# One score product per block and head in the mixed part, and a rewritten set-up of block-sparse attention with a mixture of experts

## The chip, the cores and the metric

The kernel runs on one core of one Trainium2 chip. The metric is the time of one execution on the device in microseconds (us), as the median of several runs. Profiles come from one further execution, whose times are given in us from the start of its span. Engine names are those of the profile: PE is TensorE (PEld its weight loads), DVE VectorE, ACT ScalarE, POOL GpSimd and SP the engine that issues most DMAs.

## The reference

Attention over 4 batches, 8 heads, 768 positions of 64 features, in 24 blocks of 32 positions. A query block sees its own block and both neighbours, the first and the last block, and three sampled blocks; the first and last query block see everything. The result goes, token by token, through four experts with two layers each.

```python
mask = np.abs(blk_i - blk_j) <= window
mask = mask | (blk_i == 0) | (blk_j == 0) | (blk_i == n_blocks - 1) | (blk_j == n_blocks - 1)
for qb in range(n_blocks):
    for kb in sampled_blocks[qb]:
        mask[qb*block:(qb+1)*block, kb*block:(kb+1)*block] = True
attn = softmax(np.where(mask, scale * q @ k.T, -1e9));  x = attn @ v
for e in range(E):
    h = np.maximum(x @ w1[e], 0.0)
    out += p[:, e:e+1] * (h @ w2[e])
```

## The kernel before, in words

**Tiling of the attention.** The 22 inner query blocks of a batch are gathered in groups t of four (the last has two). A group is worked on as two units u of four heads each (class `Group`), so a batch has 12 group units; the first and last query block make four `Edge` units. A query block has eight key slots of 32 positions: three neighbours (its own block and both sides), the first block, three sampled blocks, the last block. `S` (lines 292 to 323) makes the scores. For each head pair `i` and block `c` it multiplies q with the three neighbour slots, read from the batch's key tile `k` (line 304, 96 columns), and then with the other five slots, read from a buffer `kr` (line 309, 160 columns). The two heads of a pair lie in the two halves of the partitions, and the blocks' results in four groups of 32 output partitions, so eight products run side by side. Each float32 product shows as two instructions in the trace. Then DVE reduces scores and mask to a row bound (line 319) and ACT takes the exponential (322). `T` transposes the weights on TensorE (331) and copies them out (333: half on ACT, half on DVE in the set-up). `A` multiplies them with the value rows (359). In the set-up, `A` also divides by the sums (348, 349, 377), and `X` transposes a finished group into tokens (403), which `tokens` splits into high and low parts (281 on ACT, 282 on DVE) as operands of the experts.

**Buffers and loads.** `copy_k` fills the five-slot buffers `kr`: the end blocks by one copy (149), the sampled ones by one copy each (156) on POOL, ACT and DVE in turn (`copier`). Their block numbers are loaded into an engine's register on first use (141). `load_v` fetches value rows: one DMA on SP's queue for the neighbours (175) and an indirect one on POOL's queue per block for the sampled rows (179). `put_ends` copies the end rows into each value tile (852). Expert weights come by SP (580, 585) and are split into high and low parts by ACT and POOL (597 and 598, 611 and 612, 635 and 636).

**Order of the work.** All engines run in the order in which the code issues instructions. The kernel has two parts. The set-up and the first six units of batch 0 (lines 833 to 898) run alone, since the experts need tokens. The mixed part begins with the first expert product (662) and interleaves expert products (662, 683, 732) with the other attention units by planned times (`drive`, `attend`). The planned times depend on constants of the code. In `attend`, unit n's scores are issued in iteration n, its transposes and values in iteration n + 1. The slots of the next group are copied in two portions: one block's in the iteration of the first unit of a group, the other three blocks' in that of the second; there are five `kr` buffers in this part and eight in the set-up.

The mask is made from `bad` (which slots to drop) by one small product with a pattern of 24 x 768 elements, `ind` (239 to 258).

## Time and profile before

| what | value |
|---|---|
| median of 3 runs | 1254.86 us (1254.47 to 1259.41) |
| profiled execution | 1257.47 us, its span 1255.6 us |
| mean granted TensorE clock | 0.995 |
| keys of batch 0: first copies that read them start at | 8.94 us |
| mean of one exponential on ACT (L322, 128x256) | 499 ns |
| starts of score units around a refill of keys, batches 0 and 1 | 115.39 and 127.00; 136.87 and 148.77; 240.51 and 252.57; 264.18 and 274.05; 285.69 and 297.32; 309.67 and 321.30; 332.91 and 342.81 us |
| the closest such pair in batches 2 and 3 | 480.81 and 495.60 us |

How to read it: the span goes from the first to the last instruction; the time of the execution has some 2 us more. A stage in which an engine is busy all the time is bound by that engine. The TensorE clock has two levels here, 1.0 (2.4 GHz) and 0.5 (1.2 GHz). In a row of the timeline, the first number is the start, the second how long the instructions in the row were busy; the time from one row's start to the next is what the work costs when rows follow without idle time.

### The profile page before, as it was taken

To read this page: it belongs to the slowest core of one execution; us is meant where nothing else is said; L and a number is where in the kernel's file an instruction comes from. 1 tells how busy PE (TensorE), PEld (TensorE's weight loads), DVE (VectorE), ACT (ScalarE), POOL (GpSimd) and SP (SyncE) were. 2 spreads that over 40 slices of the span, in tenths; PEclk is the share of its full clock that TensorE was granted. 3 is DMA by queue.
4 is the path that set the end of the run, shared out by engine and by line. 5 is a ranking of instruction groups with operands and counts; after the bars stand their busy time and mean duration, and the time that the engine had idled before them with its cause. 6 is when DMAs were issued, how large, how long until landed. Compare 5 with 4: busy or idle time off the path is not lost.

```text
span 1255.6 us, 31597 instructions
## 1 busy us (share of the span) xinstructions
PE 1231.8 (98%) x12242; PEld 1072.5 (85%) x12242; DVE 753.9 (60%) x1735; ACT 679.5 (54%) x1826; POOL 719.0 (57%) x848
## 2 busy tenths in 40 slices
PE   6899999999999999999999999999999999999998
PEld 4788888888888888888888888888888899999997
DVE  6455535555458675666658676665756855555553
ACT  5556645666655546666555455666664544444441
POOL 6566556666659545555547655556544855555550
PEclk9899999999999999999999999999999999999999
DMA  9546555655535325332323433333321222222211
GB/s 258 181 128 170 153 183 170 192 174 173 159 111 188 110 68 156 98 118 90 111 86 120 145 102 100 103 119 114 118 77 43 93 93 67 68 68 68 67 51 51
DMA packets 64113, 149.02 MB, mean 119 GB/s; under 512 B 7707, under 2 KB 9244, under 8 KB 63964
## 3 DMA queue, kind: packets, MB, share of 16 engines
q1 hardware_dynamic: 58294, 129.70, 32.9%
q0 software_dynamic: 5632, 17.31, 5.1%
q8 instruction: 96, 1.57, 0.5%
q14 instruction: 53, 0.43, 0.1%
q10 hardware_dynamic: 38, 0.00, 0.0%
HBM read 140.69 MB, written 6.29 MB: 117 GB/s over the span
## 4 chain that ended last, share of the span: by engine, by line
PE 67%; DVE 1%; issue 1%; POOL 0%; POOLq 0%; DVEq 0%
PE po L732 33%; PE w L683 16%; PE v L683 12%; PE o L359 2%; PE tp L331 1%; PE s L309 1%; PE s L304 1%; DVE oacc L747 1%; PE ow L469 1%; PE sw L418 1%; PE tw L440 0%; DVE r L619 0%; POOL wo L612 0%; DVE r L617 0%; PE v L662 0%
## 5 line engine op out<-in xcount | busy, mean ns | idle before, releaser
L612 POOL TENSOR_TENSOR wo<-r,wo 128x256 fp32r<-128x256 f32 x288 | 241.1, 840 | 279.7 <-ACT wo L611 278.1
L732 PE MATMUL po<-h,hh 128*128 128x512 f32 x768 | 310.2, 404 | 1.3 <-DVE oacc L747 1.1
L732 PE MATMUL po<-h,hl 128*128 128x512 f32 x768 | 302.6, 394 | 0.0
L732 PE MATMUL po<-l,hh 128*128 128x512 f32 x768 | 301.7, 393 | 0.0
L683 PE MATMUL w<-xo,wo 128*128 128x384 f32 x1152 | 236.1, 340 | 0.0
L636 POOL TENSOR_TENSOR l<-r,h 128x512 fp32r<-128x512 f32 x160 | 211.4, 1321 | 37.5 <-ACT h L635 37.0
L683 PEld LDWEIGHTS w<-xo,wo 128*128 128x128 f32 x1152 | 207.5, 188 | 18.0 <-DVE z L718 0.7
L683 PE MATMUL v<-xo,wo 128*128 128x384 f32 x864 | 175.9, 338 | 0.0
L732 PEld LDWEIGHTS po<-h,hl 128*128 128x128 f32 x768 | 144.2, 188 | 33.0
L683 PEld LDWEIGHTS v<-xo,wo 128*128 128x128 f32 x864 | 154.4, 188 | 12.3 <-ACT z L710 0.2
L732 PEld LDWEIGHTS po<-h,hh 128*128 128x128 f32 x768 | 144.2, 188 | 19.6 <-DVE oacc L747 2.9
L598 POOL TENSOR_TENSOR wo<-r,wo 128x256 fp32r<-128x256 f32 x128 | 95.3, 747 | 114.7 <-ACT wo L597 109.3
L732 PEld LDWEIGHTS po<-l,hh 128*128 128x128 f32 x768 | 145.2, 189 | 11.4
L611 ACT CAST wo<-r 128x256 fp32r<-128x256 f32 x288 | 114.5, 398 | 49.7 <-PE w L683 32.2
L747 DVE SCALAR_TENSOR_TENSOR oacc<-po,pr,oacc 128x512 f32<-128x512 f32 x168 | 124.3, 742 | 24.6 <-PE po L732 24.4
L322 ACT ACTIVATE p<-p,mx 128x256 f32<-128x256 f32 (+1 forms) x192 | 95.5, 499 | 69.4 <-DVE mx L319 67.5
L635 ACT CAST h<-r 128x512 fp32r<-128x512 f32 x160 | 99.3, 620 | 11.8 <-PE po L732 11.8
L179 POOL DMA_INDIRECT v<-in_vr_dram,vidx x88 | 85.7, 974 | 26.3 <-issue 16.6
L319 DVE CUSTOM_DVE_ANT_1 p<-s,mask 128x256 f32<-128x256 f32 (+1 forms) x192 | 69.9, 418 | 46.3 <-PE s L309 45.9
L662 PE MATMUL v<-xo,wo 128*128 128x384 f32 x384 | 79.9, 345 | 0.5 <-ACT xo L281 0.5
L706 DVE TENSOR_TENSOR p<-w,p 128x384 f32<-128x384 f32 x48 | 26.7, 556 | 89.4 <-PE w L683 82.3
L662 PE MATMUL w<-xo,wo 128*128 128x384 f32 x384 | 79.1, 341 | 0.0
(139 smaller groups left out, 1723.4 us busy)
## 6 DMA issues: line engine op xcount, KB each, us to landing
r<-in_w_dram SPq DMA_DIRECT2D x80, 512.0 KB, 4.0
r<-in_w_dram SPq DMA_DIRECT2D x160, 256.0 KB, 2.7
v<-in_vr_dram SPq DMA_DIRECT2D x44, 384.0 KB, 4.8
k<-in_kb_dram SPq DMA_DIRECT2D x8, 768.0 KB, 5.7
v<-in_vr_dram SPq DMA_DIRECT2D x12, 512.0 KB, 5.1
out_dram<-oacc SPq DMA_DIRECT2D x23, 256.0 KB, 2.5
q<-in_qb_dram SPq DMA_DIRECT2D x20, 256.0 KB, 5.2
v<-in_vr_dram SPq DMA_DIRECT2D x24, 128.0 KB, 3.4
```

What stands on the lines that cost most here:

```text
L179: nc.gpsimd.indirect_dma_start(out=v[:G, i, 1], out_offset=None, in_=vr, element_offset=b * S * DM, in_offset=bass.IndirectOffsetOnAxis(ap ...
L319: nc.vector.tensor_tensor_reduce(p.rearrange("p (a b) -> p a b", b=BLOCK), s[h][:n, i], mk, -SCALE, 3.0e38, ALU.add, ALU.min, mx[:n])
L322: nc.scalar.activation(p, p, AF.Exp, bias=mx[:n], scale=-1.0, accum_out=self.sums[:n, m:m + 1])
L598: nc.gpsimd.tensor_sub(o[:, 1], r[s][:, i, k], f32(o[:, 0]))
L611: nc.scalar.copy(o[:, 0], src)
L612: nc.gpsimd.tensor_sub(o[:, 1], src, f32(o[:, 0]))
L635: nc.scalar.copy(h, r)
L636: nc.gpsimd.tensor_sub(l, r, f32(h))
L662: nc.tensor.matmul(W[s], w[:, wi, t], x[xi][:, k * KH + t], start=k == 0 and m == 0, stop=k == 1 and m == 3 * KH - 1)
L683: nc.tensor.matmul(ps, w[:, wi, t], x[:, xi, t], start=fresh and m == 0, stop=m == 3 * KH - 1, skip_group_check=not fresh)
L732: nc.tensor.matmul(p, a[:, js], w, start=f == 0 and n == 0, stop=f == FT - 1 and n == 2)
L747: nc.vector.scalar_tensor_tensor(accs[tok], p, pe, accs[tok], op0=ALU.mult, op1=ALU.add)
```

## The change

In the mixed part a `kr` buffer has all eight slots: the three neighbours come by a DMA of their own on SP's queue, and `S` makes one product of 256 columns for a block and head. There are four such buffers instead of five, and the slots of all four blocks of the next group are filled in the iteration of the group's second unit. The five-slot form and two products stay in the first six units. There, keys of four blocks lie in one buffer (two of them), with one copy for all end blocks; block numbers are loaded early; ACT and POOL do most sampled copies; the end rows are copied by halves of the heads. `S` and `soft` are split, so that TensorE's instructions of an iteration come before the softmax of the same unit, and the half copy of the unit before lies between the exponentials. Division (`G`) and token split (`C`) are issued after the softmax. The third group's value loads come ahead of the second w1 load and the w2 loads. The mask is made by two smaller products. Some small tiles have fewer buffers, and the edge queries share the ring of the q tiles and are loaded in the mixed part.

```diff
-        return nc.scalar if j <= QG and r == 2 else COPIERS[r % len(COPIERS)]
+        if first_units[0]:
+            if j <= QG:
+                return (nc.gpsimd, nc.scalar, nc.vector if j % 2 else nc.scalar)[r]
+            return nc.gpsimd if (j + r) % 2 else nc.scalar
+        return COPIERS[r % len(COPIERS)]
...
+    def read_blocks(t, eng):
+        for j in blocks(t):
+            for r in range(NR):
+                if copier(j, r) is eng:
+                    sampled_block(j, r)
...
     def copy_k(b, t, cs=range(QG)):
         for c, j in enumerate(blocks(t)):
             if c in cs:
+                w = pool["slots"] - NR - 2
...
                 k = keep("k", make)
+                if w:
+                    nc.sync.dma_start(k[:, :w], kb[b, :, j - 1:j + 2])
...
-                    copy(k[:, 1 + r:2 + r], keys[b][0][:, bass.ds(sampled_block(j, r), 1)])
+                    copy(k[:, w + 1 + r:w + 2 + r], keys[b][0][:, bass.ds(sampled_block(j, r), 1)])
...
+    def group_keys(t):
+        ks = kept.get(t % 2) or pool["k"].tile([P, QG, NR + 2, P], F32, name="kr")
+        if t < 2:
+            kept[t] = ks
+            nc.vector.tensor_copy(ks[:, :, 0:NR + 2:NR + 1],
+                                  keys[0][0][:, 0:NB:NB - 1].unsqueeze(1).broadcast_to([P, QG, 2, P]))
+        gathered[0, t][1].update((c, ks[:, c]) for c in range(QG))
...
-    for c in range(QG):
-        for r in (1, 2):
-            sampled_block(1 + c, r)
+    for t in range(2):
+        read_blocks(t, nc.scalar)
...
                     for h, half in enumerate(halves):
-                        nc.tensor.matmul(s[h][cs, i, :3], q[half, c, e], k[half, j - 1:j + 2, e],
-                                         start=True, stop=True)
-                for c, j in enumerate(blocks(t)):
+                        if whole:
+                            nc.tensor.matmul(s[h][cs, i], q[half, c, e], ks[c][half, :, e],
+                                             start=True, stop=True)
+                        else:
+                            nc.tensor.matmul(s[h][cs, i, :3], q[half, c, e], k[half, j - 1:j + 2, e],
+                                             start=True, stop=True)
+                for c, j in enumerate(() if whole else blocks(t)):
...
+                if i == 0 and between:
+                    between()
...
-        renew(2 * QG, 4)
+        pool["slots"] = SLOTS - 3
+        renew(0, 4)
...
+        read_blocks(0, nc.gpsimd)
         load_v(0, 0, (0, 1))
-        copy_k(0, 0)
-        make_identity(nc, ident)
...
+        load_v(0, 0, (2, 3), (True, False))
+        kept["vi"] -= 1
+        read_blocks(0, nc.vector)
+        load_q(0, 1)
+        for t in range(2):
+            group_keys(t)
+            if t == 0:
+                for eng in COPIERS:
+                    copy_some(0, eng)
+                make_identity(nc, ident)
+                load_v(0, 0, (2, 3), (False, True))
+        copy_some(1, nc.scalar)
+        copy_some(1, nc.gpsimd)
+        for n in range(2):
+            put_ends(n, 0)
+        load_v(0, 1)
         us = units(0)
+        copies = {}
+        for n in range(NG + 2):
+            if n < NG:
+                us[n].S()
+            if n >= 2:
+                us[n - 2].A()
+            if 4 <= n < NG + 1 and n % 2 == 0:
+                us[n - 3].X()
+            if 1 <= n <= NG:
+                copies[n - 1] = [us[n - 1].T(i) for i in range(2)]
+            if n < NG:
+                us[n].soft(copies[n - 1][0] if n else None)
+            elif n == NG:
+                copies[n - 1][0]()
+            if n in (2, 3, 4):
+                for i in range(2):
+                    put_ends(*((i, 1), (2 + i, 0), (2 + i, 1))[n - 2])
+            if n >= 2:
+                us[n - 2].G()
+            if 1 <= n <= NG:
+                copies[n - 1][1]()
+            if 4 <= n < NG + 1 and n % 2 == 0:
+                us[n - 3].C([slice(0, HP)])
             if n == 1:
                 load_q(0, 2)
+                group_keys(2)
+                load_w1(0, 0)
+                copy_some(2, nc.gpsimd)
+            if n in (2, 3):
+                copy_some(2, nc.scalar, slice(3 * (n - 2), 3 * (n - 1)))
+            if n == 3:
+                load_v(0, 2)
+                load_w1(0, 1)
                 for f in range(3):
                     load_w2(f)
...
+            if n == NG:
+                next(weights)
+                split_w2(0)
+                next(weights)
+        us[NG - 1].X()
+        us[NG - 1].C([slice(0, KH), slice(KH, HP)])
+        next(weights)
+        split_w2(1)
+        for f in range(2, 4):
+            split_w2(f)
...
-    pool["k"] = ctx.enter_context(tc.tile_pool(name="k2", bufs=5))
+    pool["k"] = ctx.enter_context(tc.tile_pool(name="k2", bufs=QG))
+    pool["slots"] = SLOTS
...
-                copy_k(b, t, (1, 2, 3) if n % 2 else (0,))
+                else:
+                    copy_k(b, t)
```

`copy_some(t, eng, some)` issues the sampled copies of group t that `copier` gives to that engine, or a slice of them.

## Rows read from the trace of the kernel before

**Rows 1.** Busy time per engine over the span, from the first part of the page.

```profile
PE 1231.8 (98%) x12242; PEld 1072.5 (85%) x12242; DVE 753.9 (60%) x1735; ACT 679.5 (54%) x1826; POOL 719.0 (57%) x848
```

**Rows 2.** Busy time in five stretches of the run. Columns: stretch, its length, busy us (instructions) on PE, PEld, DVE, ACT, POOL, granted TensorE clock, busy share of the DMA engines, GB/s.

```profile
8.40:24.70 16.30, 12.78 (x273) 8.57 (x273) 12.95 (x48) 11.70 (x41) 11.19 (x20) 0.91 1.05 268
24.70:49.20 24.50, 17.36 (x558) 14.02 (x557) 14.10 (x48) 14.87 (x45) 13.47 (x15) 0.92 0.58 164
49.20:52.50 3.30, 3.30 (x10) 3.30 (x11) 1.21 (x4) 0.78 (x2) 0.62 (x2) 0.50 0.66 168
...
170.00:400.00 230.00, 229.06 (x2688) 198.27 (x2687) 127.45 (x319) 136.65 (x375) 152.08 (x177) 1.00 0.55 174
400.00:950.00 550.00, 549.12 (x5780) 477.25 (x5779) 360.32 (x838) 321.80 (x881) 307.92 (x366) 1.00 0.35 108
```

**Rows 3.** The score instructions: from the view of line 304 after 52.5 us, the products (line 309 has the same count there); from the groups of the whole run, the weight loads of line 304 with busy us and mean ns.

```profile
L304 PE MATMUL s<-k,q x1216: 242/243/267, 104.0 to 941.3; 64*32 64x96 f32 x174
...
L304 PEld LDWEIGHTS s<-k,q 64*32 64x32 f32 x1408 | 23.6, 107 | 19.4 <-issue 10.6 <-ACT wo L597 2.9 <-ACT hh L671 2.6
```

**Rows 4.** TensorE's timeline through one score unit of four blocks in the mixed part, up to the first row of the value products behind it. Columns: start us, busy us, engine, line, operation, output and inputs, shapes, count.

```profile
309.67 0.40 PE L304 MATMUL s<-k,q 64*32 64x96 f32 x16
309.86 0.48 PE L309 MATMUL s<-kr,q 64*32 64x160 f32 x16
310.13 0.37 PE L304 MATMUL s<-k,q 64*32 64x96 f32 x16
310.29 0.58 PE L309 MATMUL s<-kr,q 64*32 64x160 f32 x16
310.81 1.10 PE L359 MATMUL o<-v,pt 128*32 128x64 f32 x64
```

**Rows 5.** The same for a unit of two blocks: its first row and the row behind it.

```profile
354.27 0.37 PE L304 MATMUL s<-k,q 64*32 64x96 f32 x8
...
355.27 0.65 PE L359 MATMUL o<-v,pt 128*32 128x64 f32 x32
```

**Rows 6.** The same for an edge unit, whose product has 384 columns.

```profile
73.83 0.88 PE L418 MATMUL sw<-k,qe 64*32 64x384 f32 x16
74.63 0.88 PE L469 MATMUL ow<-v,ptw 128*32 128x64 f32 x48
```

**Rows 7.** TensorE's and SP's timelines around the closest two score units with a refill of keys between them: the first rows of both units, and the first load that SP issues after the first of them was due.

```profile
264.18 0.40 PE L304 MATMUL s<-k,q 64*32 64x96 f32 x16
...
274.05 0.40 PE L304 MATMUL s<-k,q 64*32 64x96 f32 x16
...
266.88 0.37 SPq L175 DMA_DIRECT2D v<-in_vr_dram  x1
```

**Rows 8.** From issue to landing: the value loads of line 175 on SP over the whole run (384 or 512 KB), and the indirect ones on POOL in the first 36 us (median us at the end of the row).

```profile
DMA to landing us min/median/max: 3.6/4.8/13.1
...
v<-in_vr_dram,vidx POOLq DMA_INDIRECT x12, 8.7
```

**Rows 9.** Loads of block numbers into ACT's registers, from the view of line 141: ns of one (least, median, most), first and last start in us.

```profile
L141 ACTq TENSOR_LOAD <-sbrow x26: 276/279/485, 2.1 to 139.6; - x26
```

**Rows 10.** POOL's timeline: the last two sampled copies of the first group, and the next indirect value load but for the identity's two steps.

```profile
10.43 1.15 POOL L156 COPY kr<-k 128x128 f32 x2 [0.34 <-issue]
...
12.27 0.97 POOL L179 DMA_INDIRECT v<-in_vr_dram,vidx  x1 [0.17 <-issue]
```

**Rows 11.** Groups of instructions over the run that give durations: busy us, mean ns of one, idle time before.

```profile
L333 ACT COPY pt<-tp 128x512 f32<-128x512 f32 x74 | 39.9, 588 | 4.2 <-PE tp L331 3.9
...
L156 ACT COPY kr<-k 128x128 f32 x104 | 25.2, 294 | 8.4 <-DMA k<-in_kb_dram 5.7 <-issue 2.3 <-ACT kr L156 0.3
...
L333 DVE COPY pt<-tp 128x512 f32<-128x512 f32 x6 | 4.1, 685 | 1.8 <-PE tp L331 1.8
L852 DVE COPY v<-ends 32x2048 f32<-32x2048 f32 x3 | 3.6, 1221 | 0.1
...
L377 DVE TENSOR_TENSOR xg<-o,rec 128x256 f32<-128x256 f32 x6 | 2.5, 425 | 1.5 <-PE o L359 1.1
```

**Rows 12.** Timeline rows of the first six units, of DVE and PE; in brackets the idle time of the engine before the row and what ended it.

```profile
13.27 0.42 DVE L319 CUSTOM_DVE_ANT_1 p<-s,mask 128x256 f32<-128x256 f32 x1 [2.07 <-PE s L309]
13.62 0.42 DVE L319 CUSTOM_DVE_ANT_1 p<-s,mask 128x256 f32<-128x256 f32 x1
...
21.46 1.41 PE L359 MATMUL o<-v,pt 128*32 128x64 f32 x50 [0.46 <-DMA v<-in_vr_dram,vidx]
...
22.80 1.97 PE L331 MATMUL tp<-ident,p 128*128 128x128 f32 x8
...
27.71 1.09 PE L359 MATMUL o<-v,pt 128*32 128x64 f32 x62 [1.32 <-issue]
...
28.73 1.09 PE L331 MATMUL tp<-ident,p 128*128 128x128 f32 x8
...
38.27 0.27 PE L304 MATMUL s<-k,q 64*32 64x96 f32 x2 [2.68 <-issue]
...
46.22 1.25 DVE L348 TENSOR_SCALAR rec<-sums 128x4 f32<-128x4 f32 x1
...
49.17 3.89 PE L662 MATMUL v<-xo,wo 128*128 128x384 f32 x12 [0.46 <-ACT xo L281]
```

More of the change, by code (lines that the diff above doesn't have):

```diff
@@ L155, in copy_k, with copy_some @@
                     copy = eng.copy if eng is nc.scalar else eng.tensor_copy
-                    copy(k[:, 1 + r:2 + r], keys[b][0][:, bass.ds(sampled_block(j, r), 1)])
+                    copy(k[:, w + 1 + r:w + 2 + r], keys[b][0][:, bass.ds(sampled_block(j, r), 1)])
                 gathered[b, t][1][c] = k
+    def group_keys(t):
[5 more added lines that the diff above has]
+        gathered[0, t][1].update((c, ks[:, c]) for c in range(QG))
+    def copy_some(t, eng, some=slice(None)):
+        copy = eng.copy if eng is nc.scalar else eng.tensor_copy
+        for c, j, r in [(c, j, r) for c, j in enumerate(blocks(t)) for r in range(NR)
+                        if copier(j, r) is eng][some]:
+            copy(gathered[0, t][1][c][:, 1 + r:2 + r], keys[0][0][:, bass.ds(sampled_block(j, r), 1)])
     def end_rows(b):
@@ L174, in load_v @@
             rows = vr[b * S + (js[c] - 1) * BLOCK:b * S + (js[c] + 2) * BLOCK]
-            nc.sync.dma_start(v[:3 * BLOCK, :n, 0],
-                              bass.AP(rows.tensor, rows.offset,
-                                      [[DM, 3 * BLOCK], [BLOCK * DM, n], [1, DM]]))
-            for i in range(n):
+            if parts[0]:
+                nc.sync.dma_start(v[:3 * BLOCK, :n, 0],
+                                  bass.AP(rows.tensor, rows.offset,
+                                          [[DM, 3 * BLOCK], [BLOCK * DM, n], [1, DM]]))
+            for i in range(n if parts[1] else 0):
                 nc.gpsimd.indirect_dma_start(
@@ L295, in S @@
             q, ks, _ = gathered[b, t]
+            whole = pool["slots"] == SLOTS
             s = [pool["s"].tile([P, HH, SLOTS, BLOCK], F32, name="s", tag="s") for _ in range(2)]
@@ L332, in T @@
                                     ident[:n, :n])
-            (pool["half"] if i else nc.scalar.copy)(self.pt[:, 4 * i:4 * i + 4, :n], tp[:, :, :n])
+            copy = lambda: (pool["half"] if i else nc.scalar.copy)(self.pt[:, 4 * i:4 * i + 4, :n], tp[:, :, :n])
+            if pool["squares"]:
+                copy()
+            return copy
         def N(self, m):
@@ L398, in X, with C @@
                     tokens(j, self.x[:, :, :n], [slice(u * HH, (u + 1) * HH)])
-            elif u:
-                x = pool["o"].tile([P, HP, P], F32, name="x", tag=pool["tag"])
-                g = self.xg.rearrange("p u a m d -> p (u a) (m d)")
-                for i in range(HP):
-                    nc.tensor.transpose(x[:, i, :n], g[:n, i], ident[:n, :n])
-                tokens(j, x[:, :, :n], [slice(0, KH), slice(KH, HP)] if parts else [slice(0, HP)])
+                return
+            self.x = x = pool["o"].tile([P, HP, P], F32, name="x", tag=pool["tag"])
+            g = self.xg.rearrange("p u a m d -> p (u a) (m d)")
+            for i in range(HP):
+                nc.tensor.transpose(x[:, i, :n], g[:n, i], ident[:n, :n])
+        def C(self, kts):
+            tokens(blocks(self.t)[0] * BLOCK, self.x[:, :, :self.n], kts)
     class Edge:
@@ L879, in attention_moe_kernel @@
                 for f in range(3):
                     load_w2(f)
-                load_edge_q(0)
-            if n == 3:
-                load_v(0, 2)
-            if n >= 2:
+            if n in (4, 5):
                 next(weights)
-            if n >= 4:
-                split_w2(n - 4)
-        us[NG - 3].X()
-        us[NG - 1].T(0)
-        us[NG - 1].T(1)
-        us[NG - 2].A()
-        us[NG - 1].A()
-        for n in range(3):
-            next(weights)
-            if n:
-                split_w2(n + 1)
@@ L897, in attention_moe_kernel @@
-        us[NG - 1].X(1)
+                next(weights)
[5 more added lines that the diff above has]
+        us[NG - 1].C([slice(0, KH), slice(KH, HP)])
+        next(weights)
+        split_w2(1)
+        for f in range(2, 4):
+            split_w2(f)
         pool["p"] = pp
```

133 lines of the change are left out of this document (67 added, 66 removed).

## The prediction

> **What bounds the kernel now.** I read the page's busy shares first [rows 1]: TensorE is busy 98% of the span. Then a table by stage [rows 2], which cuts the run in two. From 8.4 to 49.2 us only the first six attention units run: TensorE is busy 12.78 + 17.36 of 40.8 us, and the DMA engines are full up to 24.7 us. The first expert product starts at 49.17 us, where one stage ends and the other begins. Its first 3.3 us run at half clock, and from then on TensorE is busy 229.06 of 230 us and 549.12 of 550. So time is won in two ways only: fewer nanoseconds per TensorE instruction in the mixed part, or an earlier first expert product.
>
> **Part 1, the score product of the mixed part.** The change replaces two products per block and head (96 and 160 columns) by one of 256 and drops the second weight load. The mixed part holds 1,216 instructions of each form [rows 3]; a head pair of one block has four of a form, two heads in two passes each, so a unit of four blocks has 32 of each and the last unit pair of a batch half of that: 34 units of four blocks and 8 of two (34 x 32 + 8 x 16 = 1,216).
> What do columns cost? In a four-block unit [rows 4] sixteen 96-column instructions take 0.16 us (310.13 to 310.29) and sixteen of 160 take 0.27 (309.86 to 310.13): 1.7 ns per column and group of sixteen in both, with no fixed part to see. So two head pairs in one piece still stream 2 x 0.43 = 0.86 us. What is left over differs. The four-block unit takes 1.14 us from its first product to the next line's (309.67 to 310.81), 0.28 over. The two-block unit [rows 5] takes 1.00, 0.14 over; the edge score [rows 6], which does 384 columns in one product, takes 0.80 against 0.64 of streaming, 0.16 over. The unit with most instructions has the extra 0.12, and one sees where: its last group of sixteen lies stretched over 0.58 us where that of the first head pair has 0.48 [rows 4]. The changed unit has as few instructions as the two-block unit has now; I give it the edge's 0.16: 1.02 us. Saved: 34 x 0.12 = 4.1 us, and about 0 in the two-block units. As TensorE is the bound, all of it counts. Ends: 0 if the stretch stays, and 34 x 0.28 + 8 x 0.14 = 10.6 if start and tail went too. I take 4.0, nearest to the edge row.
> What it adds: three key slots of each block come by DMA, 76 loads of 192 KB in the mixed part, issued by SP at some 0.4 us each. The engines have room: 55% busy up to 400 us, then 35% [rows 2]. These loads bring a new wait: a key buffer is refilled once the second unit of a group of blocks has read it, and the next unit's scores need it. Behind the waiting load on SP's queue stand weight and value loads, and for those TensorE waits at last. The slots are due one unit later, 264.18 to 274.05 us in the tightest case seen [rows 7]. SP comes to that point 2.7 us late (266.88 [rows 7]), four issues take 1.6, and a load lands after 4.8 (the median of the value loads, twice the size [rows 8]): 9.1 us, under 9.87. I cost it at nothing; the cover is that slack, thin twice. The sampled copies keep their number; 18 more block numbers are loaded into registers in batch 1, some 0.5 us each [rows 9] on engines 55 to 66% busy there [rows 2]. One buffer less saves four copies of end blocks on POOL, off the path. The smaller rings of edge tiles, and the q ring shared with the edge queries, wait for work a whole unit earlier. Nothing for these.
>
> **Part 2, set-up and first six units.** I follow the new order with durations of before.
> (a) POOL loads its block numbers between its key copies now (0.34 us idle before the last two, which end at 11.58 [rows 10]), after the change ahead of the keys' landing at 8.94 (the table above), so its four copies end near 10.2. ACT has twelve numbers to load instead of eight, 0.28 us for the load and as much for the rest [rows 9]: from 2.1 until about 8.9, its six copies (0.29 each [rows 11]) until 10.6. The first score reduction starts at 13.27 now [rows 12], 1.7 after the last key copy; then at 12.3.
> (b) The first attention-times-value product waits for indirect value loads until 21.46 [rows 12]; POOL issues the last pair of them from 12.27 [rows 10], then 1.3 us sooner, as its copies end sooner. The pair ahead slips about as much, as the number loads stand before it, and is still the earlier one. Also, one w1 load, three w2 loads and the edge queries (1.4 MB, 5.3 us at 268 GB/s [rows 2]) no longer stand in the DMA queues there; they follow the value rows of the third group. I take 1.4 us: the product runs at 20.1, and the second unit's transposes start at 21.3 where they start at 22.80 now [rows 12].
> (c) From there I walk the chain. Unit costs [rows 4, 11, 12]: eight transposes 1.97 us at half clock and 1.09 at full, scores 1.14 (1.4 where the clock changes), values 1.1, four final transposes 0.6; on DVE four reductions 1.4 (one every 0.35), weights and product 0.9 (0.42 for the product), copy of half the transposes 0.69, two half copies of end rows 1.2; on ACT an exponential 0.5 (the table above), the other half copy 0.59, a key copy 0.29. Transposes of unit 1 to 23.3, scores 3 to 24.7, values 1 to 25.8, plus 1.0 for an issue stall (1.32 at this place now [rows 12]): 26.8; transposes 2 to 27.9. Scores 4 then wait for ACT's last key copies: half copy to 28.0, two exponentials to 29.0, copies to 29.8; the rest of the scores to 30.6; values 2 31.7, final transposes 32.3, transposes 3 33.4. Now DVE is the bound: reductions 4 from 30.8 to 32.2, end rows 33.4, weights 34.3, copy 35.0; TensorE: values 3 36.1, transposes 4 37.2. DVE again: 0.7 for the tokens' low part to 35.7, reductions 5 37.1, weights 38.0, copy 38.7; values 4 39.8, final 40.4, transposes 5 41.5; copy 42.2; values 5 43.3; weights 44.2; final 44.8; ACT's cast, for which TensorE waited 0.46 [rows 12], 45.2. With some 0.05 us for each of ten hand-overs the first expert product starts at 45.7 instead of 49.17: 3.5 us sooner. Of before's delays two go: 2.68 us of issue stall at 38.27, which the wait for DVE hides here, and the 1.25 us for a small step on DVE at 46.22 [rows 12], which now has fewer w2 splits on POOL beside it, two of four being behind the last product. Late next is DVE, 4.2 us per unit.
> Ends: TensorE alone, at full clock without waits from 21.3, needs 5 x 1.09 + 3 x 1.14 + 5 x 1.1 + 3 x 0.6 = 16.2 us, product at 37.5, 11.7 gained; at half clock 1.8 times as much, 50.5, 1.3 lost. The half clock at the start of the mixed part [rows 2] I leave as it is: what precedes it, a TensorE with gaps, stays.
>
> **Sum.** 4.0 + 3.5 = 7.5 us off the profiled execution (1257.47 us, span 1255.6). That lies 2.6 above the median of the runs, 1254.86; I take the same 7.5 off the median: 1247.4.
>
> **Rivals.** *Set-up gains nothing* (20%): loads and issue stalls set its end. For it speak the full DMA engines up to 24.7 us; against it their 58% after that [rows 2], where TensorE waits for other engines. Only part 1: 1250.9. *The fused score gains nothing* (7%): streaming is equal, and if the stretch is not from instruction count it stays: 1251.4. *Set-up gains far more* (12%), near its TensorE end, 9 us: 1241.9. *Weight loads are the true price* (4%): the loads of the first form are 23.6 us busy for 1,408 [rows 3]; without 1,216 of them that is 20.4 us less, with part 2 1231.0. Against it, time follows columns alone [rows 4]. The Trainium skill ("Trainium Kernel Development and Optimization", "Performance Expectations") says that LDWEIGHTS busy time, not matmul busy time, tells how near TensorE is to its limit. By that rule this rival would be the forecast; the trace disagrees as far as the equal ns per column go.
> *Late key slots* (8%), on the other side. The place is the score product after a refill, seven times in batches 0 and 1 where units lie 9.9 to 12.1 us apart, ten times later at 14.8 or more (the table above). If a load needs 8.7 us, as POOL's did in the full set-up [rows 8], SP's 2.7 + 1.6 + 8.7 = 13.0 us overrun the seven by 12.4 us in sum, 4.9 slower than before: 1259.8. It decides from a landing of 5.6 us in the two tight units and 7.3 in the others; 13.1, the slowest value load [rows 8], would cost some 60. The Trainium skill ("DMA: Bandwidth & Descriptors", "Issuing engines are not separate DMA queues") says that loads of all issuers share the same 16 engines and interleave. The trace agrees: 4.8 us at the median against 8.7 where the engines are full.
>
> **Chances and range.** Forecast case 49%, its own range 1244.5 to 1250.5. About 0.5% (6.3 us: below 1248.6 or above 1261.1) is what a measurement can tell from no change. Of the forecast's 49, 37 fall below 1248.6 and 12 above. Faster: 37 + 12 + 4 = 53%; slower: 5 of the late slots' 8; within: 12 + 20 + 7 + 3 = 42%. The range 1241 to 1253 leaves out the weight-load and late-slot cases and a few per cent of tails.
>
> **What would show it.** Part 1 right: from one product line to the next, a four-block score unit of the mixed part takes 1.02 us and a two-block unit 1.00; wrong: 1.14 or 0.8. There is no TensorE wait of microseconds for the keys' DMA. Part 2: first reduction at 12.3 us, first value product complete before 21, first expert product near 45.7, with DVE as releaser of TensorE's waits from unit 4 on. A first product at 49 or later, or issue stalls in the chain as long as now, would make the prediction wrong.

## The result, and the profile after

The changed kernel takes 1264.33 us (median of six runs, 1262.26 to 1266.36), the kernel before 1256.91 (six runs, 1254.47 to 1259.41): 1.0061 of it, 95% interval 1.0049 to 1.0073. It is 7.4 us slower, where 7.5 us faster was predicted. The profiled execution took 1265.44 us, its span 1263.7.

Lines moved: 304 and 309 became 346 in the mixed part (349 and 354 in the set-up), 359 is 415, 331 is 384, 662 is 724, 732 is 794, 683 is 745, 672 is 734, 636 is 698, 826 is 888, 179 is 211, 156 is 188. The busy shares [rows 1] after:

```profile
PE 1233.3 (98%) x11028; PEld 1054.9 (83%) x11028; DVE 763.0 (60%) x1741; ACT 674.4 (53%) x1815; POOL 714.5 (57%) x850
```

TensorE has 1,214 instructions less and is busy 1.5 us longer. The stages [rows 2] after, with a stretch from 58 to 65 us in the place of 49.2 to 52.5:

```profile
8.40:24.70 16.30, 10.93 (x254) 8.08 (x254) 10.49 (x36) 8.12 (x33) 12.97 (x25) 0.87 1.01 249
24.70:49.20 24.50, 18.11 (x563) 13.81 (x563) 15.80 (x51) 15.30 (x50) 9.47 (x11) 0.95 0.49 143
49.20:52.50 3.30, 3.30 (x21) 3.30 (x21) 0.42 (x1) 3.30 (x9) 2.69 (x3) 1.00 0.23 79
...
58.00:65.00 7.00, 5.87 (x19) 5.88 (x20) 2.05 (x5) 1.19 (x3) 1.46 (x2) 0.51 0.55 181
...
170.00:400.00 230.00, 228.50 (x2367) 193.01 (x2367) 127.30 (x318) 135.75 (x373) 149.59 (x177) 1.00 0.63 191
400.00:950.00 550.00, 549.00 (x5076) 467.30 (x5075) 368.18 (x839) 318.29 (x865) 308.26 (x365) 1.00 0.41 125
```

The stretch at half clock has moved from 49.2 to 58 us, behind a pause of TensorE, and become longer. What lies before it is seen in the timelines. The set-up first, TensorE but for one row of DVE (answers to [rows 12]):

```profile
12.98 0.43 DVE L370 CUSTOM_DVE_ANT_1 p<-s,mask 128x256 f32<-128x256 f32 x1 [0.43 <-PE s L354]
...
21.94 1.70 PE L415 MATMUL o<-v,pt 128*32 128x64 f32 x50 [2.00 <-DMA v<-in_vr_dram,vidx]
23.58 1.97 PE L384 MATMUL tp<-ident,p 128*128 128x128 f32 x8
...
39.32 0.28 PE L349 MATMUL s<-k,q 64*32 64x96 f32 x4 [3.42 <-issue]
...
42.31 1.29 PE L415 MATMUL o<-v,pt 128*32 128x64 f32 x64 [0.29 <-ACT pt L386]
...
45.35 1.15 PE L415 MATMUL o<-v,pt 128*32 128x64 f32 x64 [0.29 <-ACT pt L386]
...
48.62 2.46 PE L724 MATMUL v<-xo,wo 128*128 128x384 f32 x12 [0.46 <-ACT xo L321]
50.92 2.25 PE L724 MATMUL w<-xo,wo 128*128 128x384 f32 x12
59.13 4.21 PE L724 MATMUL v<-xo,wo 128*128 128x384 f32 x12 [5.96 <-DVE hl L734]
63.13 3.05 PE L724 MATMUL w<-xo,wo 128*128 128x384 f32 x12
66.02 2.24 PE L724 MATMUL v<-xo,wo 128*128 128x384 f32 x12
```

POOL in the same stretch (answers to [rows 10]), with the first and the third of the indirect value loads that the first group waits for, and the four key copies between them:

```profile
7.18 1.09 POOL L211 DMA_INDIRECT v<-in_vr_dram,vidx  x1 [3.16 <-DVE picked L294]
...
9.50 1.79 POOL L188 COPY kr<-k 128x128 f32 x4
...
12.88 0.96 POOL L211 DMA_INDIRECT v<-in_vr_dram,vidx  x1 [0.18 <-issue]
```

The first expert product comes 0.55 us sooner than before (48.62 against 49.17). Two rows of products later TensorE stands still for 5.96 us. Followed back on the other engines:

```profile
48.15 6.48 SPq L647 DMA_DIRECT2D r<-in_w_dram  x4
54.68 0.43 SPq L888 DMA_DIRECT2D pr<-in_probs_dram  x1
...
50.51 3.77 POOL L698 TENSOR_TENSOR l<-r,h 128x512 fp32r<-128x512 f32 x3
...
57.51 0.25 DVE L889 TENSOR_REDUCE psum_e<-pr 128x24 f32<-128x96 f32 x1 [7.62 <-DMA pr<-in_probs_dram]
...
58.52 0.55 DVE L734 SCALAR_TENSOR_TENSOR hl<-v,hh 128x384 fp32r<-128x384 f32 x1
```

Read from below: `hl` (the low part of the hidden activations, which frees the PSUM tile of the next expert product) stands on DVE behind the sum over the probabilities; that waits for the load of `pr`; SP issues that load behind four loads of w2 rows, and those wait for buffers which POOL frees in the three w2 splits that the change puts behind the last attention product. The first second-layer product is due at 61.22 us before and starts at 68.10 after: 0.55 us gained have become 6.88 lost.

From there to the last product another 1.8 us are lost, though the scores save some 4 us. Against before, from product to product in the 1,803 pairs of second-layer products that follow each other directly, the sum went from 425.1 to 429.1 us, the median of a step from 231 to 234 ns. The page shows it in one group:

```profile
L794 PE MATMUL po<-h,hh 128*128 128x512 f32 x768 | 313.0, 408 | 1.3 <-DVE oacc L809 1.3
L794 PE MATMUL po<-h,hl 128*128 128x512 f32 x768 | 302.9, 394 | 0.0
L794 PE MATMUL po<-l,hh 128*128 128x512 f32 x768 | 302.8, 394 | 0.0
```

Before:

```profile
L732 PE MATMUL po<-h,hh 128*128 128x512 f32 x768 | 310.2, 404 | 1.3 <-DVE oacc L747 1.1
L732 PE MATMUL po<-h,hl 128*128 128x512 f32 x768 | 302.6, 394 | 0.0
L732 PE MATMUL po<-l,hh 128*128 128x512 f32 x768 | 301.7, 393 | 0.0
```

The products are the same ones. What differs is where the hidden activations lie: the rings of the edge tiles and the edge queries' buffer were cut by 3,232 bytes, so all tiles behind them moved down by that, and the hidden activations from a multiple of 128 bytes to 32 off a multiple of 64. (Addresses are those of the built kernels.)

The scores themselves (answers to [rows 4, 5, 7]):

```profile
270.85 1.09 PE L346 MATMUL s<-kr,q 64*32 64x256 f32 x32
280.92 1.45 PE L346 MATMUL s<-kr,q 64*32 64x256 f32 x32
...
305.53 1.09 PE L346 MATMUL s<-kr,q 64*32 64x256 f32 x32
306.55 0.65 PE L415 MATMUL o<-v,pt 128*32 128x64 f32 x32
...
361.50 1.07 PE L346 MATMUL s<-kr,q 64*32 64x256 f32 x16
362.49 0.65 PE L415 MATMUL o<-v,pt 128*32 128x64 f32 x32
```

306.55 - 305.53 = 1.02 us for four blocks, 362.49 - 361.50 = 0.99 for two: what Part 1 said. Of the 42 units only the one at 280.92 is longer than its like, by some 0.36 us; the trace shows TensorE's weight loads waiting there for the keys' DMA.

### The profile page after: what moved, and what is told of

Its sections match the earlier page's. It is cut to its first block, busy times and chain, and to the rows that moved or that the text cites. A ratio compares the mean times of both kernels' runs of the same rounds, so it can differ in the third digit from the quotient of the medians.

```text
span 1263.7 us, 29421 instructions
## 1 busy us (share of the span) xinstructions
PE 1233.3 (98%) x11028; PEld 1054.9 (83%) x11028; DVE 763.0 (60%) x1741; ACT 674.4 (53%) x1815; POOL 714.5 (57%) x850
## 4 chain that ended last, share of the span: by engine, by line
PE 66%; DVE 3%; issue 0%; ACT 0%; POOL 0%
PE po L794 32%; PE w L745 16%; PE v L745 11%; PE s L346 2%; PE o L415 2%; PE tp L384 1%; DVE oacc L809 1%; DVE d L596 1%; PE ow L530 1%; PE sw L479 1%; PE tw L501 0%; DVE r L681 0%; DVE hl L753 0%; DVE xo L593 0%; DVE xr L596 0%
## 5 line engine op out<-in xcount | busy, mean ns | idle before, releaser
L745 PEld LDWEIGHTS v<-xo,wo 128*128 128x128 f32 x864 | 154.7, 188 | 12.6 <-ACT z L772 0.2
L724 PEld LDWEIGHTS v<-xo,wo 128*128 128x128 f32 x384 | 69.8, 192 | 13.7 <-DVE hl L734 6.3
```

The source lines that it names most:

```text
L724: nc.tensor.matmul(W[s], w[:, wi, t], x[xi][:, k * KH + t], start=k == 0 and m == 0, stop=k == 1 and m == 3 * KH - 1)
L745: nc.tensor.matmul(ps, w[:, wi, t], x[:, xi, t], start=fresh and m == 0, stop=m == 3 * KH - 1, skip_group_check=not fresh)
```

## Experiments

Two theories after the result. *Chain*: the late w2 splits hold SP's queue, and with it `pr`, DVE and TensorE, some 7 us. *Place*: the shifted hidden activations cost 2 to 3 ns per second-layer product, some 5 us. Against each stands that the other does it all, or that the set-up's stalls do.

The runs fell on several chips, so each is compared only with the kernel before as it ran beside it on the same chip: 1272.37 us for the first four and 1273.74 for the next four (one chip), 1255.48 for e9 to e12 (a second chip), 1256.04 for e13 to e15 (a third).

**e1, e2, e3: one cause taken away, the other, both.** In e1 the load of `pr` is issued early, in e2 two small tiles are merged, which moves the hidden activations by 32 bytes to a multiple of 64; e3 has both.

In e1, the first line taken out is that of `token_weights`:

```diff
-        nc.sync.dma_start(pr, probs)
...
                 for f in range(3):
                     load_w2(f)
+                nc.sync.dma_start(pr, probs)
```

In e2:

```diff
-            new = at.tile([P, 1, 2], F32, name="new2", bufs=1)
+            new = at.tile([P, 2, 2], F32, name="new2", bufs=1)
+            new, rec = new[:, 0:1], new[:, 1:2]
...
-            rec = at.tile([P, 1, 2], F32, name="rec1", bufs=1)
```

> Edit: the changed kernel with one DMA moved: the load of the token weights (probs) is issued on SP in the fourth attention unit, behind the first three w2 loads, instead of at the start of the mixed part, behind four further w2 loads. Theory A (SP's queue): the changed kernel's TensorE waits 5.96 us for a step on DVE at 59.13 us, DVE waits 7.62 us for that load, and SP issues it only at 54.68 because three w2 loads before it wait for POOL's splits. Then the wait goes, and with it the longer stretch at half clock: 7.4 us less (the changed kernel is 0.55 us ahead of the old one at the first expert product and 6.89 behind at the first second-layer product), 1257 us. Rival A (the work is short there anyway: the next operand, a weight or a w2 half, is as late): 3 us less at most, 1261 or more.

> Edit: the changed kernel with two 8-byte tiles of the edge units put into one, so that all tiles behind them, the hidden activations hh and hl among them, begin 32 bytes lower: at multiples of 64 bytes, as in the old kernel, and no longer 32 bytes off. Theory B (placement): the second-layer products step 2 to 3 ns slower each in the changed kernel (234 against 231 ns at the median, 2,304 of them, to the end of the run where no attention is left), because their stationary operand is read from such addresses. Then they go back to 231 ns and 5.3 us go: 1259 us. Rival B (the 76 key loads contend with the products' reads, or the runs differ by chance): no change, 1264, and 234 ns stays.

> Edit: both edits above. Theories A and B together: 7.4 + 5.3 = 12.7 us less, 1251.6 us, some 5 us under the old kernel. Rivals A and B: between 1259 and 1264.

Measured: e1 1264.49 us (0.9940, 0.9921 to 0.9959), e2 1265.31 (0.9945, 0.9927 to 0.9963), e3 1258.99 (0.9891, 0.9872 to 0.9910). On one chip, the place is worth e3 - e1 = -5.5 us and the early load e3 - e2 = -6.3, where 5.3 and 7.4 us less were expected. Each edit moves what its theory names and leaves the other: from the first expert product to the second layer there are 10.6 us in e1 and e3 and 19.4 in e2, and the second-layer sum is 429.5 us in e1 and 424.6 and 424.4 in e2 and e3. Both theories hold side by side. But all three beat the kernel before by far, which takes 15 us longer here than in the first result; that had to be understood before any sum.

**e4: the shift put into the kernel before.** 32 unused bytes among the edge tiles move all later tiles.

```diff
     at = ctx.enter_context(tc.tile_pool(name="at", bufs=2))
+    pad = at.tile([P, 8], F32, name="pad", bufs=1)
```

> Edit: the old kernel with 32 unused bytes in front of the small tiles, so that the hidden activations begin 32 bytes off a multiple of 64 as in the changed kernel; nothing else. Theory B: 5.3 us slower, 1262 us, median step of second-layer products 234 instead of 231 ns. Rival B: no change, 1256.9.

Measured: 1277.82 us, 1.0046 (1.0032 to 1.0061): 5.5 us slower, by 32 bytes that nothing reads. This kernel has none of the change's key loads, so it is not they that slow the products.

**b1, a1: both kernels, unchanged, on that chip.**

> The kernel before once more, unchanged, for its trace on the chip of the next three runs. On the first chip its span was 1255.6 us; on the second its median was 15 us longer than on the first. If a chip differs in how fast TensorE gets its instructions, the 'issue' waits of TensorE are longer there than the 1.32, 0.75 and 2.68 us of the first trace and the steps of the second-layer products stay at 231 ns. Rival: the products themselves take longer there (over 232 ns).

> The changed kernel once more, unchanged, on the same chip as the others. If the two chips differ only by an equal amount for both kernels: 1.006 of the kernel before, as on the first chip. If what the second chip costs goes with the number of TensorE instructions (12,242 before, 11,028 after), the changed kernel loses less there: 0.997 to 1.001 of the kernel before.

Measured: before 1273.74 us (16 runs), the changed kernel 1270.60, 0.9975 (0.9966 to 0.9985). Here the change is 0.25% *faster*. TensorE's waits in the kernel before, first in the trace ahead of the prediction, then on this chip (columns: line waited for, releaser, us in total, times, longest):

```profile
PE s L304 <- issue: 2.7, 1, 2.7
...
PE o L359 <- issue: 1.7, 2, 1.3
```

```profile
PE o L359 <- issue: 5.2, 10, 1.5
...
PE s L304 <- issue: 3.5, 8, 1.2
```

The same instructions come late more often, in runs of small products (scores in the set-up, values), while the second-layer steps are the same (425.3 us). From the first expert product to the last product the kernel before needs 1201.6 us in the first trace (49.17 to 1250.79) and 1211.4 here (55.73 to 1267.12). The changed kernel needs 1210.8 (48.62 to 1259.44) and 1212.6 (52.08 to 1264.69): with the 1,214 instructions it has lost, it loses 1.8 us on this chip, the kernel before 9.8. Half of the 9.8 lies at one line: the time from each value product of the mixed part to the next product adds up to 41.1 us in the first trace of the kernel before and 46.0 here, and to 40.1 and 40.7 in the changed kernel; at the scores themselves it is 46.8 us in both traces of the kernel before. The value products stand right behind the scores, which now have half as many instructions. So the sign of this change depends on the chip. Why this chip delivers instructions late, the traces don't say.

**e5, e6: the mixed part alone**, with the set-up of before; e6 also has e2's edit.

```diff
-                        nc.tensor.matmul(s[h][cs, i, :3], q[half, c, e], k[half, j - 1:j + 2, e],
-                                         start=True, stop=True)
+                        if whole:
+                            nc.tensor.matmul(s[h][cs, i], q[half, c, e], ks[c][half, :, e],
+                                             start=True, stop=True)
...
-    pool["k"] = ctx.enter_context(tc.tile_pool(name="k2", bufs=5))
+    pool["k"] = ctx.enter_context(tc.tile_pool(name="k2", bufs=QG))
```

> Only the mixed part changed: one score product of 256 columns, four key buffers of eight slots, the cut rings; the set-up as before. The hidden activations then lie 3,232 bytes lower, 32 bytes off a multiple of 64, as in the changed kernel. Theory of the place in SBUF: the score units save 4.0 us, the 2,304 second-layer products take 2 to 3 ns more and give 5.3 back: 1.3 us slower than before, steps of 234 ns. Rival, the place has no say and the loss is all at the start of the mixed part: 4.0 us faster, steps of 231 ns. If fewer TensorE instructions also save issue waits on this chip, both come out some us lower.

> As the run before it, with two small tiles of the edges in one, so that the hidden activations lie on a multiple of 64 bytes: 5.3 us faster than that run and steps of 231 ns, if their place is the cause (4.0 us faster than before, or more by what fewer instructions save). If the place has no say: the same time as that run.

Measured: e5 1266.33 us (0.9945, 0.9929 to 0.9960), e6 1260.54 (0.9895, 0.9876 to 0.9914): the place again 5.8 us, with the second-layer sum 429.3 against 424.3. Both are far below before, as the expectation's last sentence allowed: on this chip the steps at the value products, 46.0 us in the kernel before, add up to 40.2 and 39.8 in e5 and e6.

**e9: the hidden activations moved by 32 bytes**, in the kernel before. The tiles behind them move by 64 bytes and so stay on multiples of 64.

```diff
+    lo = ctx.enter_context(tc.tile_pool(name="lo", bufs=1)).tile([P, 8], F32, name="lo")
     later["h"] = ctx.enter_context(tc.tile_pool(name="hp", bufs=2 * FT))
+    hi = ctx.enter_context(tc.tile_pool(name="hi", bufs=1)).tile([P, 8], F32, name="hi")
```

> The kernel before with 32 unused bytes ahead of the hidden activations and 32 behind them: they alone lie 32 bytes off a multiple of 64, all tiles behind them on multiples of 64 as before. If their place is the cause: 5.3 us slower than before and steps of the second-layer products of 234 ns, as in the run that moved all the later tiles. Rival: the place of other tiles (queries, keys, values, transposed weights) did it: same time as before, steps of 231 ns.

Measured: 1262.73 us against 1255.48, 1.0063 (1.0049 to 1.0077): 7.2 us slower. The tiles behind the hidden activations lie 64 past a multiple of 128 in e6 too, without loss, so it is the place of the hidden activations. Second-layer products of e9:

```profile
L732 PE MATMUL po<-h,hh 128*128 128x512 f32 x768 | 311.7, 406 | 1.0 <-DVE oacc L747 1.0
L732 PE MATMUL po<-h,hl 128*128 128x512 f32 x768 | 303.9, 396 | 0.0
L732 PE MATMUL po<-l,hh 128*128 128x512 f32 x768 | 303.0, 395 | 0.0
```

The steps (sums from start to start over the pairs that follow each other directly, in us, from the traces):

| kernel | hidden activations lie | second layer, 1,803 pairs | first layer of the later sets (line 683 before, 745 in the changed kernel), 1,680 pairs |
|---|---|---|---|
| before | 0 past a multiple of 128 | 425.1 | 298.6 |
| e4, e9 | 32 past it | 429.6, 429.6 | 301.4, 301.4 |
| changed, e5 | 96 past it | 429.1, 429.3 | 298.8, 298.6 |
| e6, e12 | 64 past it | 424.3, 424.2 | 297.9, 297.8 |

For e9 the two columns give 4.5 + 2.8 = 7.3 us, near what was measured, though the sums leave out steps between products of different lines. From the first expert product to the last product e9 needs 1208.7 us in its trace, 7.1 more than the kernel before in the first. The steps were expected at 234 ns and have a median of 232 with a mean (of those under 300 ns) of 233.9; before it is 231.3. The second column is a miss of the theory: those products don't read the hidden activations, and their own operands (`xo`, `wo`) lie at the same addresses in all these kernels; they still take longer in e4 and e9, where the hidden activations lie 32 past a multiple of 128, but not in the changed kernel, where it is 96. By these runs the place of the hidden activations also costs where they are not read; by what way, none tells.

**e11, e12: with both causes mended, what is the rewritten set-up worth?** e11 is e3 again, e12 is e6 again, now side by side.

> The changed kernel with both edits once more, beside the next run. Theory: with the load chain and the place mended, what is left of the rewritten set-up is what its trace gained at the first expert product, 0.9 us against the next run; so 0 to 2 us faster than the next run. Rival, as the prediction had it: 3.5 us faster.

> Only the score product, with the set-up of before and the activations on a multiple of 64, once more: 0.9895 of the kernel before on the second chip; on a chip like the first one, where the instructions come in time, 4.0 us faster than before (0.9968).

Measured: e11 1250.38 us (0.9960, 0.9947 to 0.9974), e12 1250.60 (0.9964, 0.9950 to 0.9978). The mixed part's change alone, well placed, gives 4.9 us; the set-up on top of it 0.2, nothing that can be told from zero. e11's first expert product is 0.62 us ahead (47.05 against 47.67), its first second-layer product 1.14 (57.67 against 58.81), and then this, in e11:

```profile
60.48 1.33 PE L724 MATMUL w<-xo,wo 128*128 128x384 f32 x6 [1.96 <-DVE hl L734]
...
58.73 0.71 ACT L659 CAST wo<-r 128x256 fp32r<-128x256 f32 x2 [4.53 <-DMA r<-in_w_dram]
...
46.57 6.53 SPq L647 DMA_DIRECT2D r<-in_w_dram  x4
...
53.63 0.46 SPq L642 DMA_DIRECT2D r<-in_w_dram  x1
```

The same queue still: SP is held until 53.1 by the w2 buffers, so a w1 load goes out at 53.63, ACT gets it at 58.73, and the hidden activations, `hl` behind them and TensorE follow.

**e10: is the stall in the fifth score unit a fetch behind loads?** e3 with the second w1 load and three w2 loads where before has them, ahead of the third group's value rows.

```diff
-                load_w1(0, 0)
+                for s in range(2):
+                    load_w1(0, s)
+                for f in range(3):
+                    load_w2(f)
...
                 load_v(0, 2)
-                load_w1(0, 1)
-                for f in range(3):
-                    load_w2(f)
```

> The changed kernel with the early load of the probabilities and the aligned activations, and with the second w1 load and three w2 loads issued where the kernel before has them, ahead of the value rows of the third group. If TensorE's stall in the fifth score unit (3.42 us in the changed kernel, 2.08 with both edits) is a fetch of instructions queued behind those loads: below 1.2 us, the indirect loads of the third group land 2 us sooner after their issue, and the first expert product comes 1 us or more sooner. Rival, the value rows alone hold the fetch, or the loads have no part in it: a stall of 2 us or more, the first expert product not sooner, or later by up to 2 us because the first units' value rows share the queues.

Measured: 1250.41 us (0.9962, 0.9948 to 0.9975), the same as e11. The stall, in e11 and in e10:

```profile
36.53 0.38 PE L349 MATMUL s<-k,q 64*32 64x96 f32 x4 [3.69 <-issue]
```

```profile
26.34 1.75 PE L415 MATMUL o<-v,pt 128*32 128x64 f32 x64 [2.06 <-ACT p L373]
...
36.95 0.28 PE L349 MATMUL s<-k,q 64*32 64x96 f32 x4 [1.01 <-issue]
```

It falls from 3.69 us to 1.01 when four loads fewer are in the queues there. One trace each would be little, as the stall varies: it is 3.42, 3.69, 4.53 and 3.42 us in the four traces of the changed order on the chips without late instructions (changed kernel, e11, e13, e14), and 1.01 and 1.99 in the two with the earlier loads (e10, e15). In each of the six, one packet of 16 KB on a queue that the profile calls `instruction` ends 1.3 to 1.5 us before the stall does. That points to a fetch of instructions, and the stall is longer with the loads ahead of it. A part of it stays without them, and when the fetch was asked for, the traces don't tell. The first expert product comes 0.36 us sooner (46.69), not the 1 us expected: the units ahead wait longer instead, TensorE for ACT by 2.06 us at 26.34.

**e13, e14, e15: the splits back at their old places.** All have the aligned activations; e14 adds the early load of `pr`, e15 also e10's loads.

```diff
             if n in (4, 5):
                 next(weights)
                 next(weights)
+                split_w2(n - 4)
             if n == NG:
                 next(weights)
-                split_w2(0)
+                split_w2(2)
                 next(weights)
...
         next(weights)
-        split_w2(1)
-        for f in range(2, 4):
-            split_w2(f)
+        split_w2(3)
```

> The changed kernel with aligned activations and the w2 splits 0 to 3 at the places that the kernel before has (one in each of the last two score units, one behind each of the last two value products); the probabilities' load stays where the change leaves it. If the late splits are the root: no wait of TensorE for hl of more than 1 us between the first expert product and the first second-layer product, 1 to 3 us less than the run with both edits (about 1248 us on a chip where that takes 1250.4, 0.994 of the kernel before). Rival, the load's own place is the root: a wait of 4 us or more for hl stays and the time is that of the run with aligned activations alone, some 6 us more than with both edits.

> As the run before it, and the probabilities loaded early. If the late splits are the root, within 1 us of the run before it; if both have a part, 1 us or more faster than it.

> As the run before it, and the second w1 load and three w2 loads issued ahead of the third group's value rows. If the set-up's end is set by loads and instruction fetch: 0.5 to 2 us faster than the run before it. Rival, ACT and DVE set it: the same time within 0.5 us.

Measured: e13 1253.35 us (0.9973, 0.9963 to 0.9982), e14 1249.48 (0.9949, 0.9937 to 0.9961), e15 1247.82 (0.9932, 0.9919 to 0.9945). That the splits are the sole root is a miss: in e13 SP is still held 6.3 us by three w2 loads, `pr` goes out at 53.79, and TensorE waits:

```profile
57.78 3.67 PE L724 MATMUL v<-xo,wo 128*128 128x384 f32 x12 [3.03 <-DVE hl L734]
...
56.16 0.25 DVE L889 TENSOR_REDUCE psum_e<-pr 128x24 f32<-128x96 f32 x1 [4.69 <-DMA pr<-in_probs_dram]
```

The load's place costs 3.9 us of its own (e13 - e14, by medians; e13's runs go from 1250.34 to 1256.44, and its trace is of the longest). In e14 both waits for `hl` are gone, and 10.6 us lie between the first expert product and the second layer (45.85 to 56.48), where before has 12.05 and the changed kernel 19.48. The set-up now shows its gain: 2.3 us ahead of e12 at the second layer. At the last product e14 is 1.3 *behind* e12 (1243.31 against 1242.04; the two profiled executions took 1249.42 and 1249.54 us as a whole). Lost on the way, in e14:

```profile
274.55 0.69 PE L724 MATMUL v<-xo,wo 128*128 128x384 f32 x3 [0.28 <-issue]
...
476.55 0.89 PE L415 MATMUL o<-v,pt 128*32 128x64 f32 x32 [0.54 <-DMA v<-in_vr_dram]
...
840.65 0.32 PE L415 MATMUL o<-v,pt 128*32 128x64 f32 x8 [0.38 <-DMA v<-in_vr_dram,vidx]
```

At 477 us, as an example, e12 runs its 64 value products without a wait, and e14 waits for the value load; its lead over e12 falls by 1.0 us across that unit. Part of what the set-up wins is so given back at later loads and instruction waits. By time e14 and e15 are the best kernels of the study, 6.6 and 8.2 us under before; e15 against e14 is 1.7 us, as expected, but with intervals that overlap; and e15's trace, of its longest run (1250.89), has the first expert product at 47.30, later than e14's, so where its gain lies is not shown.

## Why the prediction was wrong

**Part 1 was right where it looked.** 1.02 and 1.00 us per unit were predicted, 1.02 and 0.99 to 1.00 measured. 34 x 0.115 = 3.9 us; and the time from each score product of the mixed part to the next product adds up to 46.8 us before, 43.2 in the changed kernel and 42.9 in e12. That e12 is 4.9 us ahead by the clock is not all due to the scores: in its trace the value products give 1.0 us too, and the expert products 2.7, with the hidden activations 64 past a multiple of 128 and not 0. The keys' loads do hold the tightest unit, by 0.36 us, and no other: the late-slot rival's place, without its price. The weight-load rival is out too: with 1,214 loads fewer PEld is busy 17.6 us less (1072.5 [rows 1] to 1054.9), and the scores gain no more than 3.9. The Trainium skill ("Trainium Kernel Development and Optimization", "Performance Expectations") names MFU (the share of the peak rate that the products reach) and the busy share of LDWEIGHTS as the measures of how near TensorE is to its limit; here the busy time of the weight loads did not tell what removing them would save.

**The step that failed first is "The smaller rings of edge tiles ... Nothing for these."** It was weighed as a question of waits alone. The cut rings move every later tile, and the place of the hidden activations costs 4.9 us in the second layer and 1.0 in the first (429.1 + 298.8 against e12's 424.2 + 297.8), 5.5 to 5.8 by the runs; against the kernel before, with its own good place, the two columns give 4.2 (425.1 + 298.6). It eats the saving of the scores whole. A trace of the kernel before can't show it; the change of tile sizes can be read in the diff.

**The second is the w2 splits.** The prediction counts the later splits only as relief for a step on DVE ("fewer w2 splits on POOL beside it"). It did not ask, as it did for the key loads, what on SP's queue waits for POOL to free a w2 buffer. Each split issues the load three ahead of it; behind four of them stood `pr`. The kernel before has the same order, and SP waits there too, but is through sooner:

```profile
44.86 4.84 SPq L585 DMA_DIRECT2D r<-in_w_dram  x3
49.76 0.42 SPq L826 DMA_DIRECT2D pr<-in_probs_dram  x1
```

There `pr` goes out 0.6 us after the first expert product (49.17), in the changed kernel 6.1 after it (54.68 and 48.62). Cost: 7.4 us between the first expert product and the second layer (19.48 against 12.05), of which 5.96 is the wait. The rest is mostly the half-clock stretch, which was to stay "as it is": it now follows the pause and lies over two rows of twelve products (59.13 to 66.02, 6.9 us, where rows at full clock take 2.08 each), where before has it in one (49.17 to 52.90, 3.7 us). By the runs 6.3 us go with the early load alone.

**The third is the size of Part 2.** (a) First reduction 12.98 us, not 12.3. (b) Values of unit 0 waited 2.00 us for indirect loads until 21.94, not done at 20.1; transposes at 23.58, not 21.3: 2.3 us late. The pair of loads ahead did slip (7.18, where before has 5.52), but it held POOL until 9.49 and the key copies behind it until 11.29, not 10.2; so the last pair went out from 12.88, 0.6 later than the 12.27 of before and not 1.3 sooner. (c) The issue stall of 2.68 us "which the wait for DVE hides here" came as 3.42 and was hidden by nothing, which the prediction had named as a sign of being wrong: DVE was not the bound there. Behind the stall a unit takes 3.0 us (42.31 to 45.35) with ACT as releaser, where 4.2 with DVE was forecast. 45.7 + 2.3 = 48.0, and the stall, less what the shorter units give back, makes the 48.62. In e14 the same six units end at 45.85, the time forecast, but with a stall of 3.42 us that the walk did not have, so that agreement is in part luck. The executions also differ by some microseconds in the set-up (the one before: 49.17 here, 47.40 in e9), and what is gained there partly comes back as waits later, which the sum did not allow for: by time the mended set-up is worth 0.2 us (e11 - e12), and with splits and loads moved as well 2 to 4 (e14 and e15 against e12, by their ratios on different chips; the intervals of e14 and e12 overlap).

The sum by what was measured: -4.9 (mixed part, well placed) + 5.5 to 5.8 (place) + 6.3 (chain) - 0.2 (set-up) = 6.7 to 7.0 us; measured 7.4. The terms come from two chips, each with an interval of some two us either way, so that they meet so closely is partly luck. Of the rivals "set-up gains nothing" was right for its part, and "late key slots" came nearest in time (4.9 us slower) by a mechanism that cost 0.36 us; none had either cause of the loss.

## What to carry to other kernels

When a change cuts or grows a buffer, compare the addresses of the tiles that the busiest products use, before and after; a shift of 32 bytes was worth more here than the change itself, and merging two small tiles mended it. When a step that frees a buffer is moved later, follow the queue of the engine that issues the refill: everything behind that load is moved too, whatever it belongs to. And a gain ahead of a long stage that is bound by one engine may come back as waits for that stage's loads, as in e14.

## What was not expected of the hardware

- Hidden activations 32 bytes off a multiple of 64: second-layer steps of 232 to 234 ns at the median against 231, 7.2 us in e9. 0 and 64 past a multiple of 128 are both good; 64 is 1.7 us better in the sums of the table, though the kernels differ in more than that. Why such a place costs time is not shown.
- The same kernel takes 1255 to 1257 us on three occasions and 1273 on one chip, with equal product steps there and more TensorE waits for instructions (5.2 us in ten waits at the value products against 1.7 in two). A change that removes instructions is worth more on such a chip: e6 gave 13.2 us there, e12, the same kernel, 4.9 on another.
- An instruction wait of 3.69 us fell to 1.01 when four weight loads were issued earlier (3.4 to 4.5 in four traces, 1.0 and 2.0 in two). The Trainium skill ("DMA: Bandwidth & Descriptors", "Issuing engines are not separate DMA queues") says that the DMAs that the engines issue run on the same 16 DMA engines and interleave; it does not speak of the transfers of instructions, and that these are held up by loads is what the lengths of the stall suggest.
